# Signed-square keys, the last variance on VectorE, a late set of eight tiles and a fixed order table in a two-layer linear-attention kernel

## The chip, the cores and the metric

The kernel runs on one core of one Trainium2 chip. The metric is the device time of one execution in microseconds (us). Most statements below rest on one profiled execution of each kernel, whose span runs from its first to its last instruction. The span is shorter than the device time by about 1.8 us for the kernel before. PE is TensorE, DVE is VectorE, ACT is ScalarE, POOL is GpSimd, and SP is the engine whose queue issues most of the transfers.

## The reference

The input is x, 2048 tokens of 512 values in bf16. Four blocks follow one another, each applied to a layer-normalised x and added to x: linear attention, experts for two tokens, and the same two again with the same weights.

```python
def _A_ref(x, wqkv, wo):                       # linear attention, 32 heads of 16
    q, k, v = split(x @ wqkv)
    phi = lambda t: where(t > 0, t + 1, exp(t)) + 1e-6
    pq, pk = phi(q), phi(k)
    kv = einsum("bhsd,bhse->bhde", pk, v)      # summed over all tokens
    z = einsum("bhsd->bhd", pk)
    o = einsum("bhqd,bhde->bhqe", pq, kv) / (einsum("bhqd,bhd->bhq", pq, z)[..., None] + 1e-6)
    return merge(o) @ wo

def _B_ref(x, w_r, w_gate, w_up, w_down):      # two tokens of 2048
    r = x @ w_r
    idx = argsort(-r)[:2]
    y = (silu(x[idx] @ w_gate) * (x[idx] @ w_up)) @ w_down * sigmoid(r[idx])
    return x + scatter(y, idx)

x = x + _A_ref(layernorm(x)); x = x + _B_ref(layernorm(x))
x = x + _A_ref(layernorm(x)); x = x + _B_ref(layernorm(x))
```

As written, the router sees the normalised x, and its two winners need the scores of all tokens. So the kernel ends with a chain of small steps: the last tile's variance, the last keys, the top two, the gathering of two rows, two small products, and the store of the two rows.

## The kernel before

x lies in 16 tiles of 128 tokens. Every piece of work is an `op` on one engine, with a duration assumed. A planner sorts the ops, and each engine then runs its own list in that fixed order.

```python
class Plan:
    WEIGHTS = {'phi_raw0': -3.7, 'kw_one0': 3.8, ...}       # priorities; cut

    # loads, all on SP's queue but for wk; 'after' is the planner's earliest time
    for k in range(0, NC, 2):
        dma(wk[:, k : k + 2, :], A_wk[:, k : k + 2, :], [("wk", k)], 256, eng="ACT")
    ...
    for dst, src, key, kb, after in ((wq, A_wq, "wq", 512, 8.0), (wr, B_wrc, "wr", 1, 9.0), (wot, A_wot, "wot", 512, 30.0),
                                     (wv, A_wv, "wv", 512, 30.0 + 0.5), (wo, A_wo, "wo", 512, 30.0 + 3.0)):
        dma(dst[:], src, [key], kb, after)

    def trans(t):      # the normalised tile, transposed by a transfer on SP's queue
        nc.sync.dma_start_transpose(out=xnT[:, :, t * P : (t + 1) * P], in_=xn[:, t, 0:D])

    def Q(n):          # one quarter of the queries of four tiles: needs wq and four transposed tiles
        for i in range(NC):
            T_.matmul(p()[:], lhsT=wq[:, i, c, :], rhs=xnT[:, i, j * D : (j + 1) * D], start=(i == 0), stop=(i == NC - 1))

    def O(layer, t):   # one output tile; the very last one in three column parts of one PSUM tile
        cuts = [0, 256, 384, 512] if split else [0, D]
        ...            # DVE then adds it to x and sums the row in the same instruction
        # last tile: three squares on ACT, small sums on DVE, then Ln and Exp on ACT give rho = 1/sqrt(var)

    def lin(lo, hi):   # router scores of tiles lo to hi; rc is the score before the division by the deviation
        tiny([lambda: V.tensor_tensor(out=key_hi(1)[:, lo:hi], in0=rc[:], in1=rho[:, 2, lo:hi], op=ALU.mult)], ...)

    topk(1, 0, 12)     # top-8 of the early twelve tiles, beside the last output tiles
    for _ in range(12):        # dummy matmuls that keep PE busy beside the chain
        pe(MM, lambda: T_.matmul(sp_()[:], lhsT=warm[:, 0:P], rhs=warm[:], start=True, stop=True), ...)
    topk(1)            # then the top-8 of all
    # output tiles 4 to 15 scaled on ACT, DVE and POOL; three stores of four tiles; the row's store waits for all
```

Of the kernel before, what the change touches and what calls it, by code (L numbers as in the profile page):

```python
# [16 lines left out]
P = 128  # L17
# [4 lines left out]
NF = 11  # L22
# [3 lines left out]
XW = 544  # L26
G3 = 3 * P + 1
# [22 lines left out]
class Plan:  # L50
# [3 lines left out]
    WEIGHTS = {'phi_raw0': -3.7, 'kw_one0': 3.8, 'kv1': -2.2, 'den1': -3.8, 'mid_chain0': -4.9, 'lin1': 2.2, 'consts0': 5.8, 'phi0': 0.9, 'row_sums0': -8, 'K0': -0.9, 'O1': -0.3, 'copy_ps0': 5.0, 819: -3.0, 6: 0.7, 223: -0.4, 619: -0.7, 'mid': -8, 662: -1.5, 154: 1.5, 461: -0.7, 567: 0.7, 312: -0.4, 702: -0.7, 'stats0': 2.6, 601: -0.4, 378: 0.3, 725: -6.3, 789: -4.5, 879: -2.6, 215: 0.7, 660: -3.7, 231: -0.3, 430: -1.1, 67: -3.3, 21: -3.0, 186: 2.7, 917: -3.0, 630: 4.5, 765: -3.0, 448: 1.5, 271: -4.5, 393: 3.0, 788: -1.5, 416: -3.0, 419: 3.0, 650: -2.3, 937: -0.7, 701: -5.2, 10: -3.0, 354: 1.5, 148: 1.5, 474: 2.7, 793: 0.8, 'copy_ps1': 8, 812: -0.7, 610: -0.8, 606: 3.0, 53: -1.0, 598: 0.3, 208: -1.2, 516: -3.0, 76: 0.7, 205: -0.7, 749: -3.0, 56: -3.4, 54: -0.8, 119: -2.2, 411: -0.3, 684: 0.3, 335: 0.7, 83: 3.7, 623: 0.3, 863: -0.7, 743: -0.7, 90: 2.7, 944: -0.8, 198: 3.0, 434: 0.3, 338: 1.5, 132: 0.4, 278: 0.3, 490: 1.1, 925: 3.0, 717: -3.0, 676: 3.0, 364: -0.7, 697: -0.7, 563: 2.0, 848: -0.3, 535: 0.3, 802: -0.7, 435: 0.0, 636: -0.8, 572: 1.2, 446: 0.3, 821: -0.7, 918: -2.7, 342: 2.4, 907: -3.0, 674: -3.0, 503: -0.3, 898: -3.0, 501: 0.3, 740: 1.2, 605: 0.7, 578: -0.7, 806: -2.7, 203: -0.3, 589: -1.5, 835: -3.0, 417: -1.5, 665: -3.0, 813: 3.0, 596: 3.7, 399: -2.7, 333: -3.7, 551: -3.0, 107: -0.4, 562: 0.0, 649: 3.0, 872: 3.0, 458: -1.5, 887: -1.5, 382: 3.0, 451: 1.5, 428: 0.7, 373: 0.3, 582: 3.0, 96: 0.0, 44: 1.0, 785: 0.0, 645: -6.7, 934: 0.7, 940: -6.0, 'den0': -3.2, 576: 0.7, 'finish_sums1': -6.8, 423: -0.7, 168: 0.0, 844: -1.5, 685: -3.3, 415: -1.8, 309: 1.5, 149: -4.4, 719: -0.4, 926: 2.7, 518: 1.5, 282: 3.0, 62: 1.5, 1: 1.5, 185: -0.7, 392: 3.0, 306: -0.4, 212: 0.7, 60: 2.2, 337: 1.5, 447: 1.5, 5: -0.3, 396: 1.8, 838: 3.0, 164: -3.0, 363: 0.3, 126: -1.0, 478: -0.3, 300: -1.0, 395: 4.5, 742: 0.7, 55: 2.3, 626: -1.5, 460: 0.7, 873: -0.3, 497: 1.5, 664: -2.2, 261: 3.0, 110: 0.7, 173: 0.0, 866: -0.3, 573: 1.4, 269: -0.7, 521: -0.7, 255: 3.8, 721: 0.4, 699: -0.7, 'finish_sums0': -2.1, 339: 0.7, 520: 1.5, 877: -1.9, 588: 3.0, 616: -3.3, 170: -0.7, 943: 4.8, 557: 3.0, 360: 0.3, 193: 0.3, 496: -3.0, 723: 0.3, 250: -0.3, 45: 0.0, 317: 2.7, 58: -1.5, 900: 0.3, 194: -1.5, 542: 0.3, 529: 2.2, 919: 3.0, 239: 0.7, 522: 1.5, 407: -0.3, 651: 0.7, 449: 0.3, 804: 1.5, 608: 0.3, 669: 0.3, 483: -1.5, 914: -1.5, 754: 0.7, 859: -1.5, 'pre0': -2.7, 539: 3.0, 268: 4.8, 675: 0.7, 408: -1.5, 618: -0.7, 289: 1.5, 182: -0.7, 519: -0.8, 498: 1.0, 481: -4.5, 655: -0.3, 889: -1.0, 575: -0.3, 493: 1.5, 155: -2.3, 99: -1.4, 121: -0.7, 15: 3.7, 343: -2.2, 196: -0.7, 784: 0.4, 199: 0.7, 29: -0.3, 341: 0.3, 648: -3.7, 307: 3.3, 657: -3.0, 732: -0.7, 923: 0.7, 677: 2.2, 35: -1.5, 219: 1.8, 241: -0.8, 752: 3.3, 320: -1.5, 875: -3.0, 318: -0.3, 913: 3.0, 147: -1.5, 111: -1.5, 127: -0.7, 191: -2.2, 'phi_raw1': -0.9, 642: -0.6, 604: -3.0, 748: 0.7, 14: -0.3, 113: 3.0, 'topk1': 2.8, 262: 0.3, 144: -0.7, 172: 0.8, 210: 0.7, 105: -1.5, 667: -3.0, 506: -4.0, 'K_raw0': -1.9, 505: -0.3, 64: -0.3, 178: -0.3, 492: 0.3, 703: 0.3, 455: -0.7, 308: 1.5, 477: 0.7, 175: 0.3, 874: -1.5, 566: -4.5, 673: -0.7, 'Q1': -0.7, 'tail': 8, 254: -4.5, 187: -0.7, 264: 3.0, 97: 1.5, 927: -0.8, 183: 0.7, 776: 0.3, 592: 3.0, 329: -0.3, 'trans0': -6.7, 201: -3.0, 357: 0.8, 544: -0.8, 729: 1.5, 'gate_up0': 1.8, 'kw_one1': 4.5, 870: -2.1, 'mid_chain1': -3.5, 437: -0.3, 26: -0.3, 310: -0.6, 641: 0.3, 162: 1.8, 163: -1.8, 'last_scales1': 2.7, 607: 0.0, 422: -0.7, 74: 1.5, 'norm0': 0.7, 824: 3.0, 823: 0.7, 560: 0.3, 643: 0.3, 348: -3.0, 902: -0.3, 769: -3.0, 32: 0.7, 114: 0.7, 495: 0.7, 843: 2.3, 204: 3.0, 820: 0.7, 627: -0.3, 160: -3.0, 248: -0.3, 893: 3.0, 355: 3.0, 895: 3.7, 425: -0.7, 694: -0.3, 771: -1.5, 671: 3.0, 892: -3.0, 728: -0.3, 661: 0.7, 758: -2.2, 756: 0.7, 837: 0.3, 894: -0.3, 726: -0.3, 30: 0.3, 753: 0.3, 847: -0.3, 230: 0.7, 293: -0.3, 577: 0.7, 'logits0': -4.8, 359: 3.0, 849: -0.3, 406: 0.7, 181: 1.5, 540: 0.7, 140: 1.5, 871: -0.3, 603: -3.7, 450: 2.3, 635: 0.3, 901: 2.7, 561: 0.3, 639: -0.3, 381: 0.3, 34: -0.7, 731: -1.5, 23: -3.0, 757: 0.3, 600: 0.7, 376: -0.7, 922: 1.5, 27: 1.5, 243: -0.7, 103: -1.5, 779: -0.7, 897: 3.0, 825: 0.8, 445: 1.8, 'gate_up1': 7.2, 509: 3.0, 883: -0.7, 750: -1.5, 180: 3.0, 'picks0': -3.3, 273: 0.3, 693: -1.5, 854: 1.5, 558: -0.3, 939: -0.7, 475: 0.3, 20: 0.6, 'trans1': -2.5, 397: 0.7, 'rstd1': 0.3, 'rstd0': -1.0, 724: -3.0, 85: -0.7, 713: 0.7, 286: -3.0, 876: -0.7, 152: 1.5, 532: 1.5, 'patch': -1.2, 936: 0.7, 543: -0.3, 547: 0.3, 517: 1.5, 195: -0.3, 28: -0.3, 564: 3.0, 'picks1': -0.2, 385: -3.0, 375: -0.7, 916: 0.7, 534: -0.7, 9: 0.7, 'logits1': -2.7, 794: 0.3, 690: -3.0, 624: -3.0, 712: 3.0, 18: 0.3, 384: -1.2, 'K_raw1': 3.0, 799: 3.0, 891: -3.0, 700: -0.7, 292: 2.7, 476: 0.7, 'kv0': 2.7, 334: 3.0, 167: -0.7, 297: 0.7, 380: 0.3, 294: -3.0, 'wk_center0': -1.4, 68: -3.0, 109: 1.5, 369: 0.3, 862: 3.0, 770: -1.5, 511: -0.3, 'norm1': -1.5, 311: -3.0, 25: -1.5, 'O0': -0.7, 761: -3.0, 929: 1.5, 546: 3.0, 453: 3.0, 'phi1': 3.0, 734: -3.0, 766: -3.0, 41: -3.0, 256: -0.7, 244: 0.7, 'last_scales0': 1.5, 814: 0.3, 464: 0.7, 'Q0': 0.7, 512: -1.5, 344: -0.7, 358: -0.7, 429: 3.0, 'K1': 0.7, 670: 0.7, 508: -2.7, 510: -0.3, 'lin0': 0.7, 480: 0.3, 533: 0.7, 'stats1': 3.0, 161: -3.0, 'G1': 0.3}  # L54
    LAT = {"PE": 0.21, "ACT": 0.16, "DVE": 0.14, "POOL": 0.1, "SP": 2.7}

    def __init__(self, slots):
        self.ops, self.wrote, self.read, self.free = [], {}, {}, dict(slots)
        self.n, self.side, self.lazy, self.bias, self.kind = 0, False, 0.0, 0.0, ""

    def op(self, eng, dur, fn, r=(), w=(), hold=(), lat=None, prio=0.0, port=False):
        prio += self.bias + self.WEIGHTS.get(self.kind, 0.0) + self.WEIGHTS.get(self.n, 0.0) + 1e-4 * self.n
        o = Op(eng, dur, self.LAT[eng] if lat is None else lat, fn, prio, port)
        self.n += 1
# [50 lines left out]
    def order(self):  # L115
        ready = []
# [13 lines left out]
        while left:  # L130
# [15 lines left out]
            if o.kb:  # L146
                bw = max(bw, o.done) + o.kb / 284.0
                o.done = bw
            elif o.queue:
                o.done = max(o.done, bw + 0.5)  # L150
# [24 lines left out]
def linear_attention_moe(  # L175
# [37 lines left out]
    xt = big.tile([P, NC, NR * P], BF16, name="xt")  # L213
# [14 lines left out]
    def dma(dst, src, keys_, kb, after=0.0, eng="SP", **k):  # L228
        e = nc.sync if eng == "SP" else nc.scalar
        o = op(eng, 0.5, lambda: e.dma_start(out=dst, in_=src), w=keys_, lat=1.7, **k)  # L230
        o.kb, o.avail = kb, after
# [4 lines left out]
    def xt_load(lo, hi, after=0.0, **k):  # L236
        dma(xt[:, :, lo * P : hi * P], A_xt[:, :, lo * P : hi * P], [("xt", t) for t in range(lo, hi)], 128 * (hi - lo), after, **k)

    for k in range(0, NC, 2):
        dma(wk[:, k : k + 2, :], A_wk[:, k : k + 2, :], [("wk", k)], 256, eng="ACT")  # L240
    op("ACT", 1.28, lambda: nc.scalar.preload_act_table_set("natural_log_exp_and_others"), w=["table"])
    for i, (load, lo, hi, after) in enumerate((
        (x_load, 0, 2, 0.0),
        (xt_load, 0, 2, 0.0),
        (x_load, 2, 4, 0.0),
        (xt_load, 2, 4, 0.0),
        (x_load, 4, 6, 0.0),
        (xt_load, 4, 6, 0.0),
        (x_load, 6, 8, 5.0), (xt_load, 6, 8, 5.0), (x_load, 8, 12, 3.5),
    ) + tuple((xt_load, lo, min(lo + 4, NR), 11.0) for lo in range(8, NR, 4)) + ((x_load, 12, 16, 13.0),)):  # L250
        load(lo, hi, after, prio=-50.0 + i)
# [85 lines left out]
    def dve(dur, fn, **k):  # L337
        return op("DVE", dur, fn, **k)
# [1220 lines left out]
```

## Time and profile before

| | |
|---|---|
| median of three executions | 158.29 us (157.55 to 159.09) |
| profiled span | 156.9 us |
| first query product | 25.52 |
| first output product of the second layer | 124.00 |
| end of the last output product on PE | 142.33 |
| sum of tile 14 read on DVE (D14) | 141.55 |
| last top-8 starts (K) | 145.60 |
| row's store issued | 153.72 |

The rows from the third on are times from the span's start in the profiled execution. D14 and K are used throughout: D14 is when VectorE has read the row sums of the last full tile, and K is when the last top-8 starts. From the page come the busy time of each engine and the row of granted PE clock in 40 equal slices, in tenths of full speed:

```profile
PE 147.9 (94%) x1380; PEld 74.4 (47%) x1380; DVE 130.2 (83%) x481; ACT 111.9 (71%) x272; POOL 28.5 (18%) x78
PEclk9999999999999999999999999999999999999996
```

From about 12 us to the end of the outputs PE is idle only in short gaps, and its granted clock is 1.00 from 12 to 150 us. DVE is nearly as full at the end: the chain of what ended last runs over DVE from 128.10 to 141.90 us, with small gaps. The prediction shows the waits and the rest of the chain. This profiled execution took 158.73 us; spans of other executions of this kernel lie between 155.4 and 157.5 us. So a difference between two kernels in the milestones below, which compares one execution of each, carries some half a microsecond of scatter.

### The profile page before, as it was taken

To read this page: it belongs to the slowest core of one execution; us is meant where nothing else is said; L and a number is where in the kernel's file an instruction comes from. 1 tells how busy PE (TensorE), PEld (TensorE's weight loads), DVE (VectorE), ACT (ScalarE), POOL (GpSimd) and SP (SyncE) were. 2 spreads that over 40 slices of the span, in tenths; PEclk is the share of its full clock that TensorE was granted. 3 is DMA by queue.
4 is the path that set the end of the run, shared out by engine and by line. 5 is a ranking of instruction groups with operands and counts; after the bars stand their busy time and mean duration, and the time that the engine had idled before them with its cause. 6 is when DMAs were issued, how large, how long until landed. Compare 5 with 4: busy or idle time off the path is not lost.

```text
span 156.9 us, 3902 instructions
## 1 busy us (share of the span) xinstructions
PE 147.9 (94%) x1380; PEld 74.4 (47%) x1380; DVE 130.2 (83%) x481; ACT 111.9 (71%) x272; POOL 28.5 (18%) x78
## 2 busy tenths in 40 slices
PE   6989999997999999999999999999999999998970
PEld 2434444443454444444545545576444455465660
DVE  1799999776699999999999979853488999999840
ACT  3379999653567788799978657712478998898930
POOL 7801055100000000120321000300430000643200
PEclk9999999999999999999999999999999999999996
DMA  3999846549998000033144530000000000030570
GB/s 103 355 355 322 241 97 71 102 100 289 439 437 340 3 4 0 0 69 67 38 102 100 105 67 6 0 4 0 0 4 0 4 0 0 4 136 2 174 231 2
DMA packets 24499, 17.15 MB, mean 109 GB/s; under 512 B 17952, under 2 KB 22560, under 8 KB 24096
## 3 DMA queue, kind: packets, MB, share of 16 engines
q1 hardware_dynamic: 24184, 16.39, 35.7%
q10 hardware_dynamic: 296, 0.53, 0.9%
q8 instruction: 10, 0.16, 0.4%
q14 instruction: 9, 0.07, 0.2%
HBM read 10.62 MB, written 2.10 MB: 81 GB/s over the span
## 4 chain that ended last, share of the span: by engine, by line
PE 72%; DVE 12%; DMA 5%; ACT 5%; issue 3%; SPq 0%; ACTq 0%; DVEq 0%
PE mm L487 18%; PE g L473 17%; PE g L618 11%; PE mm L441 10%; DVE x L628 4%; PE mm L454 4%; DMA wv<-in_A_wv_dram 3%; ACT pk L1334 3%; DMA x<-in_A_x_dram 3%; DVE st L358 2%; DVE pq L604 2%; PE tp L581 1%; PE tp L1059 1%; PE g L563 1%; PE mm L597 1%
## 5 line engine op out<-in xcount | busy, mean ns | idle before, releaser
L408 ACT ACTIVATE e<-mm 128x512 bf16<-128x512 f32 x52 | 30.4, 597 | 12.7 <-PE mm L441 6.7
L473 PE MATMUL g<-pk,xn 128*128 128x512 bf16 x128 | 32.0, 379 | 0.4 <-DVE pk L432 0.4
L487 PE MATMUL mm<-xnT,wq 128*128 128x512 bf16 x128 | 31.9, 379 | 0.0
L618 PE MATMUL g<-KW,pq 128*128 128x512 bf16 (+2 forms) x136 | 30.6, 366 | 0.4 <-DVE x L628 0.4
L636 ACT ACTIVATE sq<-x 128x512 bf16<-128x512 bf16 (+2 forms) x34 | 20.4, 601 | 2.9 <-DVE x L628 2.5
L441 PE MATMUL mm<-wk,xnT 128*128 128x512 bf16 x80 | 19.9, 379 | 0.0
L473 PEld LDWEIGHTS <-xn 128*128 128x128 bf16 x128 | 12.1, 98 | 15.9 <-issue 2.5
L618 PEld LDWEIGHTS <-pq 128*128 128x128 bf16 x136 | 12.7, 98 | 13.8 <-issue 0.5
L412 DVE TENSOR_SCALAR em<-e 128x512 bf16<-128x512 bf16 x52 | 15.1, 297 | 3.7 <-ACT e L408 3.5
L487 PEld LDWEIGHTS <-wq 128*128 128x128 bf16 x128 | 11.4, 97 | 12.5 <-issue 0.8
L394 POOL TENSOR_SCALAR xn<-x,s,nb 128x512 bf16<-128x512 bf16 x6 | 4.9, 825 | 52.9 <-PE g L618 37.9
L419 DVE SCALAR_TENSOR_TENSOR pk<-mm,em 128x512 bf16<-128x512 f32 x20 | 13.7, 687 | 0.3
L358 DVE BATCH_NORM_STATS2 st<-x 128x6 f32<-128x512 bf16 x16 | 10.4, 666 | 3.3 <-DMA x<-in_A_x_dram 3.3
L628 DVE SCALAR_TENSOR_TENSOR x<-x,opr,g 128x512 bf16<-128x512 bf16 (+2 forms) x18 | 11.9, 684 | 0.4 <-PE g L618 0.3
L441 PEld LDWEIGHTS <-xnT 128*128 128x128 bf16 x80 | 7.4, 98 | 8.9 <-DMA xnT<-xn 0.5
L628 DVE SCALAR_TENSOR_TENSOR x<-x,g 128x512 bf16<-128x512 bf16 x16 | 10.9, 683 | 0.7 <-PE g L618 0.3
L419 DVE SCALAR_TENSOR_TENSOR pq<-mm,em 128x512 bf16<-128x512 f32 x16 | 10.7, 685 | 0.1
L411 ACT ACTIVATE rl<-mm 128x512 bf16<-128x512 f32 x16 | 9.4, 612 | 1.8 <-DVE pq L416 1.0
L604 DVE TENSOR_TENSOR pq<-pq,rd 128x1024 bf16<-128x1024 bf16 x16 | 10.4, 686 | 0.0
L454 PE MATMUL mm<-wkc,xt 128*128 128x512 bf16 x40 | 10.1, 379 | 0.3 <-ACT rl L428 0.3
L427 ACT ACTIVATE e<-mm,rho 128x512 bf16<-128x512 f32 x12 | 8.2, 683 | 1.2 <-PE mm L460 1.1
L373 ACT ACTIVATE lnv<-mv,eps_t 128x2 f32<-128x2 f32 (+3 forms) x18 | 5.2, 291 | 5.0 <-DVE mv L359 3.3
(263 smaller groups left out, 232.1 us busy)
## 6 DMA issues: line engine op xcount, KB each, us to landing
wgu<-in_B_wgu_dram SPq DMA_DIRECT2D x2, 1408.0 KB, 13.6
out_dram<-pk SPq DMA_DIRECT2D x4, 512.0 KB, 4.0
wd<-in_B_wd_dram SPq DMA_DIRECT2D x1, 1408.0 KB
x<-in_A_x_dram SPq DMA_DIRECT2D x4, 256.0 KB, 5.2
xt<-in_A_xt_dram SPq DMA_DIRECT2D x4, 256.0 KB, 5.3
x<-in_A_x_dram SPq DMA_DIRECT2D x2, 512.0 KB, 5.6
wk<-in_A_wk_dram ACTq DMA_DIRECT2D x2, 256.0 KB, 4.1
wq<-in_A_wq_dram SPq DMA_DIRECT2D x1, 512.0 KB, 6.8
```

The lines of the kernel that those rows point to most:

```text
L358: dve(0.61, lambda: V.bn_stats(out=st()[:], in_=x[:, t, :]), r=[("x", t)], w=[st]).early = 4.0
L408: act(0.5, lambda: A.activation(out=e()[:], in_=p()[:], func=ACT.Exp), r=[p], w=[e], **k)
L412: dve(0.2, lambda: V.tensor_scalar(out=em()[:], in0=e()[:], scalar1=1.0, scalar2=TINY, op0=ALU.min, op1=ALU.add), r=[e], w=[em], port=True ...
L419: dve(0.6, lambda: V.scalar_tensor_tensor(out=out_ap, in0=p()[:], scalar=0.0, in1=em()[:], op0=ALU.max, op1=ALU.add), r=[p, em], w=[key], **k)
L441: T_.matmul(p()[:], lhsT=xnT[:, c, t * P : (t + 1) * P], rhs=wk[:, c, :], start=(c == 0), stop=(c == NC - 1))
L454: T_.matmul(p()[:], lhsT=xt[:, c, t * P : (t + 1) * P], rhs=w[:, c, :], start=(c == 0), stop=(t >= NM and c == NC - 1),)
L473: T_.matmul(Gs[c]()[:], lhsT=xn[:, t, gcol(c) : gcol(c) + P], rhs=pk[:, t, :], start=first, stop=last)
L487: T_.matmul(p()[:], lhsT=wq[:, i, c, :], rhs=xnT[:, i, j * D : (j + 1) * D], start=(i == 0), stop=(i == NC - 1))
L604: dve(0.6, lambda q=q: V.tensor_tensor(out=q, in0=q, in1=rd()[:].to_broadcast([P, 2, D]), op=ALU.mult), r=[rd], w=[("pq", j, c), ("pq", j, ...
L618: T_.matmul(p()[:, a : a + n], lhsT=pqt(c, t * P, P), rhs=KWs[layer][:, c, a : a + n], start=(c == 0), stop=(c == NC - 1),)
L628: dve(0.04 + 0.6 * n / D, lambda q=q, a=a, n=n: V.scalar_tensor_tensor(out=x[:, t, a : a + n], in0=x[:, t, a : a + n], scalar=1.0 if i == ...
L636: act(0.1 + 0.5 * n / D, lambda q=q, a=a, n=n, sq=sq: A.activation(out=sq()[:, 0:n], in_=x[:, t, a : a + n], func=ACT.Square, scale=float( ...
```

## The change

The intent was to close PE's two gaps, to shorten the chain behind the last tile, and to keep DVE and POOL apart in ops that the code marks `port`: in the kernel before, one clamp of 128x512 took 1.04 us on DVE at 27.29, beside memsets on POOL, where the nine others of its line took 0.25 to 0.29. The core of the diff, cut:

```diff
-    WEIGHTS = {'phi_raw0': -3.7, ...}
+    WEIGHTS = {}
+    TIMES = [0.7, 1.2, 1.7, 0.8, ..., 12.9234, 13.9234, 17.0434, 13.4236, ...]   # one start time for each op
     def order(self):
+        if self.TIMES:
+            for o in self.ops:
+                o.start = self.TIMES[o.n]
+            return sorted(self.ops, key=lambda o: o.start)
...
-    xt = big.tile([P, NC, NR * P], BF16, name="xt")
+    xt = big.tile([P, NR // 2, NC, 2 * P], BF16, name="xt")
...       # wk in two halves on two queues, x 0-1 second on ACT's queue
-    QA, QT = 3, 8
+    QA, QT = 4, 6
...       # port=True on some two dozen more ops: the table was made with DVE and POOL apart in those
-        cuts = [0, 256, 384, 512] if split else [0, D]
+        cuts = [0, 320, 512] if split else [0, D]
+        parts = [(i, a, b - a, ps("g")) for i, (a, b) in enumerate(zip(cuts, cuts[1:]))]
...       # the last part's sum of squares on DVE; variance vv without ACT
+            tiny([
+                lambda: V.scalar_tensor_tensor(out=r2[:], in0=rc[:], scalar=-1.0, in1=rc[:], op0=ALU.mult, op1=ALU.max),
+                lambda: V.tensor_tensor(out=r2[:], in0=r2[:], in1=rc[:], op=ALU.mult),
+            ], r=[("rc", lo)], w=[("r2", lo)])
+            tiny([lambda: V.reciprocal(out=iv[:], in_=vv[:])], r=["vv"], w=[("iv", lo)])
+            tiny([lambda: V.tensor_tensor(out=key_hi(1)[:, lo:hi], in0=r2[:], in1=iv[:], op=ALU.mult)], ...)
...       # key = rc*|rc|/var: the same order as rc/sqrt(var), with no Ln and Exp
-    lo, LE = ORD[12], (0, 12) if ORD[12] == 12 else (4, 16)
+    lo, LE = ORD[12], (0, L0)          # L0 = 8: early set 0-7, late set 8-15
...
-        pe(MM, lambda: T_.matmul(sp_()[:], lhsT=warm[:, 0:P], rhs=warm[:], start=True, stop=True), ...)
+        pe(0.11, lambda: [
+            T_.matmul(sp_()[:], lhsT=warm[:, 0:P], rhs=warm[:, 0:P], start=True, stop=True) for _ in range(2)
+        ], ...)
...       # gather in two halves; gate, up and down products in parts; Silu's table load earlier
```

The times of the table decide only the order.

## The prediction

> **What bounds the kernel now.** I read the page first: TensorE (PE) is busy 94% of 156.9 us, VectorE (DVE) 83%, ScalarE (ACT) 71%, GpSimd (POOL) 18%. A mean over stages decides nothing, so next came the table of busy time by stretches (start, busy us and count per engine, PE clock, DMA share, GB/s).
>
> ```profile
> 8.00:12.00 4.00, 3.37 (x16) 1.35 (x15) 4.00 (x13) 2.94 (x7) 0.09 (x1) 1.00 1.10 359
> 12.00:30.00 18.00, 18.00 (x85) 8.16 (x84) 17.55 (x59) 16.94 (x37) 6.11 (x10) 1.00 0.74 169
> 34.00:39.00 5.00, 3.87 (x19) 1.70 (x18) 3.94 (x9) 2.40 (x5) 0.00 (x0) 1.00 0.79 233
> 132.00:142.00 10.00, 9.60 (x96) 5.47 (x95) 10.00 (x45) 8.84 (x29) 5.05 (x15) 1.00 0.16 55
> 150.00:157.00 7.00, 2.12 (x88) 1.60 (x83) 1.56 (x9) 0.56 (x3) 0.00 (x0) 0.80 0.26 86
> ```
>
> There are three stages. Until 12 us loads, DVE and PE wait for each other. From 12 to 142 us PE is never idle but for two gaps. After 142 us a chain of small steps runs to 156.9: 15 us in which no engine is the bound. "Busy" alone can mislead for pipelined matmuls, so I checked the chain of work: there a group of four 512-column matmuls takes 0.86 us, 0.216 each, one after another through the whole middle. No reordering shortens that; it can only close gaps. PE's waits name all gaps over 0.35 us:
>
> ```profile
> PE tp L792 <- DMA wv<-in_A_wv_dram: 1.1, 1, 1.1
> PE g L1482 <- issue: 0.6, 1, 0.6
> PE g L1482 <- DVE h L1470: 0.5, 1, 0.5
> PE g L618 <- DVE x L628: 0.4, 1, 0.4
> PE g L473 <- DVE pk L432: 0.4, 1, 0.4
> ```
>
> The first, at 38 us, is the load of wv, issued only at 34.29 behind DMA transposes and landing 4.6 us later. The fourth, at 141.95, is the last O tile: its three column parts share one PSUM tile. The end of the chain (start us, us, what):
>
> ```profile
> 142.37 0.50 DVE x L628 x2
> ...
> 143.65 0.29 ACT sq L636 x2
> ...
> 144.80 0.30 ACT lnv L657
> 145.11 0.02 issue
> 145.13 0.20 ACT rho L660
> 145.33 3.52 ACT pk L1334 x5
> 148.86 0.02 issue
> 148.88 1.28 ACT L1447
> 150.16 0.01 issue
> 150.17 0.21 ACT s L1448
> ...
> 151.64 0.69 PE g L1482 x36
> 152.32 0.57 issue
> 152.89 0.32 PE g L1482 x8
> ```
>
> The last key needs the last tile's variance, so a square, a Ln and an Exp on ACT precede it. The timeline has the key product (L700) at 145.40 and the local top-8 (L974) at 145.60. ACT then scales five output tiles and only afterwards loads the Silu table.
>
> [...] the same clamp of 128x512 bf16 takes 350 ns in 12 to 30 us, with GpSimd a third busy, and 287 ns in 40 to 60 us, with GpSimd idle. [...] Here the load takes 1283 ns and Tanh starts 1.29 us after its beginning[...]. [...] The trace has 355 to 361 GB/s while loads saturate and 317 to 348 during the stores.
>
> **The change part by part.**
>
> *Start.* wk goes on two queues ahead of x, so the first statistics should start about 1 us later than the present 4.79. In return DVE loses work before the first pk: blockmask (0.66), casts (0.3), an xn now on GpSimd (0.39), and the order puts K of tile 7 in front of G of tile 0, where PE now waits 0.4. xt comes in 2 KB runs instead of 512 B, but loads already run at 355 GB/s. One spin less lies before work that waits for wk anyway. I count 0, give or take 0.5.
>
> *Middle.* The same matmuls of 0.216 us. The table puts wv's load ahead of wot, and the matmul that needs it well over 5 us after it: more than the 4.6 us of landing. **−1.1 us.** The last O tile gets one PSUM tile per part: **−0.4 us.** [...] Against this, DVE (17.55 of 18, and 10.0 of 10) and ACT (16.94 of 18) have hardly any slack, and all engines run a new fixed order, worked out with assumed durations. I allow **+0.5 us** of new stalls.
>
> *From tile 14 to the last keys.* Tile 14's sum ends on DVE at 141.55; the top-8 starts at 145.60, 4.05 us later. After: two x parts of 320 and 192 columns (from the rows 0.34, 0.48 and 0.74 us for 128, 256 and 512 columns, 0.08 for each accumulator: 0.63 + 0.49), mean 0.2, square-sum of 192 columns on DVE 0.5, variance 0.25, reciprocal 0.2, key 0.2, and 0.3 for the sums of tiles 12 to 14 in between (a dependent small DVE step is 0.2 from start to start, an independent one 0.1). That is 2.8; ACT's square of tile 14 and of the first part fit beside it. Ln and Exp leave this path. **−1.25 us.**
>
> *From the top-8 to the final store.* Before: top-8 at K = 145.60, row store issued at 153.72, K + 8.12. After, by engines: the top-8 over partitions 0.2 sooner, as a warm-up matmul no longer blocks it (K to the index compare 1.45, not 1.68); compare to gather 0.22; two half gathers of 16 matmuls, 0.45 each, because the late set is 8 tiles, not 4, though the add of the first half hides; gate matmuls from about K + 2.7 (was K + 3.02) with 1.29 to the first DVE step, 0.44 to Silu. So Silu starts near K + 4.4 (was K + 4.75). The steps from Silu to the down projection shrink from 1.29 to about 1.1 and the down projection comes in two parts. The up projection's second half ends near K + 5.1 and allows its share of the down projection at K + 5.7; it ends near K + 6.4, the row is ready near K + 6.7, and the store could go at K + 6.95. The 0.57 us "issue" hole inside the down projection may recur: K + 7.5. The table load moves off ACT's output queue, but Silu's input is ready at 150.31 against a table at 150.16, so this alone gives nothing.
>
> The row store must also wait for the four tile stores. Before, three of 512 KB go out at 146.12 to 148.9, and their data flow from 147 to 151.6:
>
> ```profile
> 147.00:148.00 1.00, 0.92 (x19) 0.50 (x17) 0.97 (x8) 1.00 (x2) 0.17 (x1) 1.00 0.96 317
> 150.00:151.00 1.00, 1.00 (x44) 0.97 (x39) 0.73 (x6) 0.56 (x3) 0.00 (x0) 1.00 1.03 348
> 151.00:152.00 1.00, 0.51 (x32) 0.37 (x34) 0.54 (x4) 0.00 (x0) 0.00 (x0) 1.00 0.70 224
> ```
>
> 1.5 MB at 340 GB/s is 4.6 us. The new order lets the first of these three stores go about 1.4 us after the top-8 (before: 0.5), so they would land near K + 7.5. Both paths meet there: **−0.6 us** instead of −1.2. The store, landing and end of 3.2 us stay.
>
> Sum: −1.1 − 0.4 + 0.5 − 1.25 − 0.6 = −2.85; 158.29 − 2.85 = 155.4 us.
>
> **The rivals.** *A: the fixed order stalls PE.* For it: DVE, ACT and PE are all over 94% busy in 12 to 30 us, first statistics come later, and G now trails K by two tiles, not three. Against: G's order is free, the PSUM pools are unchanged, and PE already runs ahead of DVE by a buffer or two. It would cost 1 to 3 us and leave 156 to 158.5. *B: the output stores take the place of the chain.* For it: the 4.6 us of flow above, with only about 1 us of slack now, and the later first store. It would cap the gain after the top-8 at 0.3 to 0.6, as I assume half-way; were it absent, 154.8. *C: PE was the bound and the tail's gain is all there is*, because the wv gap is only moved (the following Q and G need what DVE has not finished; DVE is 3.94 of 5 busy around the gap): 156.5. *D: everything in the sum comes without new stalls and the issue hole goes too*: 153.7.
>
> **Range and chances.** A and C are the likelier departures upward, D downward. 8 in 10: 153.6 to 157.3. A gain of 2% needs 155.13, just below my figure, so faster and same are nearly even: faster 0.45, same 0.51, slower 0.04 (a stall of over 6 us would be needed to lose 2%).
>
> **What would show it.** PE's waits without wv, PE full from about 12 us, and tile 14's sum done near 140.5 instead of 141.55 would confirm the middle; a new PE wait on pk, xn or a PSUM buffer would show A. Top-8 2.8 us after that sum, with no Ln or Exp in between, confirms the keys. A last wait of the row store on the tile stores confirms B; a wait on yo refutes it. I am wrong if PE starts its full stretch over 1 us later, or if small steps on a full DVE queue up ahead of the key.

The sum is −2.85 us and so 155.4 us; a term of 0 is cut from it. That term was an estimate of mine from 350 and 287 ns: with DVE and POOL kept apart, some 60 ns less on each of 12 clamps and less on others, about 1 us of DVE in a stretch where PE is full, and so nothing for the whole. The load of 1283 ns is ACT's table load at 148.88. The durations in the part on tile 14 that were not measured as such (mean, square-sum, variance, reciprocal, key and sums) are estimates of mine from the steps measured there: 0.2 us for a small dependent one, 0.34 to 0.74 us for one of 128 to 512 columns.

## The result, and the profile after

The changed kernel is correct and took 164.14 us (median of 4 executions, 163.44 to 164.72), against 158.11 us for the kernel before in the same rounds (157.55 to 159.09, 4 executions). The ratio is 1.0372, with a 95% interval of 1.0303 to 1.0442: slower, and far outside the predicted range. A ratio here is the mean time of one kernel's fast runs over the mean of the other's of the same rounds, so it is not quite the ratio of the medians quoted. Executions over 1.5% slower than the fastest of the same kernel are left out of the means.

The profiled span grew from 156.9 to 161.5 us; the rest of the 6.0 us is taken up under e5. By milestones, in us from the span's start:

| | before | after | difference |
|---|---|---|---|
| first query product | 25.52 | 23.94 | |
| last output product ends on PE | 142.33 | 145.23 | +2.90 |
| D14, sum of tile 14 read | 141.55 | 146.30 | +4.75 |
| K, last top-8 starts | 145.60 | 149.65 | D14 to K: −0.70 |
| row's store issued | 153.72 | 158.40 | K to store: +0.63 |
| end | 156.90 | 161.51 | store to end: −0.07 |

The four steps from D14 on sum to the +4.6 us of the span. The page of the changed kernel, same two lines as before:

```profile
PE 148.8 (92%) x1370; PEld 75.9 (47%) x1390; DVE 132.6 (82%) x486; ACT 110.1 (68%) x266; POOL 31.9 (20%) x80
PEclk9999995999999999999999999999999999999998
```

The seventh slice of the clock row says 5: half speed from 24.12 to 27.54 us from the start. PE's waits in the changed kernel (engine, line, what it waited for: us in total, times, longest) name no wv any more, and no PSUM wait at the last tile:

```profile
PE mm L502 <- issue: 2.6, 2, 2.5
...
PE tp L602 <- DVE Z L534: 0.5, 1, 0.5
```

But a wait of 2.5 us stands in front of a query product (L502). "Issue" means that the profile found no releaser, so the transfers had to be looked at. The SP queue of the changed kernel (start, us, what, count):

```profile
14.57 2.57 SPq L417 DMA_TRANSPOSE xnT<-xn  x2
17.20 0.57 SPq L240 DMA_DIRECT2D wq<-in_A_wq_dram  x1
17.86 6.44 SPq L417 DMA_TRANSPOSE xnT<-xn  x5
```

In the kernel before, wq's load was issued at 6.98. Here it stands behind two more loads and three transposes, at 17.20, and lands at 22.23. The transpose of tile 2 is issued behind it at 17.86 and lands at 23.73, 5.9 us later; the median of such a transpose is 2.5 us. The first query product needs both, and starts at 23.94, where PE was ready at 21.48. The table by stretches shows what followed (start and end, length, busy us and count of PE, PEld, DVE, ACT and POOL, then granted PE clock, DMA share, GB/s):

```profile
22.00:23.00 1.00, 0.00 (x0) 0.00 (x0) 1.00 (x7) 0.78 (x2) 0.00 (x0) 1.00 1.97 132
...
24.00:25.00 1.00, 1.00 (x3) 0.34 (x4) 0.00 (x0) 0.00 (x0) 0.00 (x0) 0.56 1.23 253
25.00:26.00 1.00, 1.00 (x4) 0.43 (x3) 0.00 (x0) 0.32 (x1) 0.00 (x0) 0.50 0.09 18
26.00:27.00 1.00, 1.00 (x4) 0.33 (x3) 0.29 (x1) 1.00 (x4) 0.00 (x0) 0.50 0.00 0
```

After the gap PE is busy, but at half clock: four matmuls take 1.71 us, not 0.86. The end of the chain of waits (start, us, what) is the second finding:

```profile
141.90 2.00 DVE x L647 x6
143.90 0.60 DVE rho L740 x2
...
144.97 1.33 DVE x L647 x4
146.30 0.08 DVE s L1022
...
149.44 0.17 DVE keys L737
...
149.69 0.14 DVE s L1022
```

From 139.45 us to K every link of it is DVE. In the kernel before, PE's last output product was still a link at 141.95. D14 now comes 1.07 us after PE's last output product, where it came 0.78 us ahead of it. The third finding is a wait of SP for the stores of the tiles, ahead of the row's store:

```profile
SPq L1584 <- DMA out_dram<-pk: 1.1, 1, 1.1
```

The row was ready at 157.09; its store went at 158.40.

### The profile page after: what moved, and what is told of

It reads as the page before. It is cut to its first block, busy times and chain, and to the rows that moved or that the text cites. A ratio compares the mean times of both kernels' runs of the same rounds, so it can differ in the third digit from the quotient of the medians.

```text
span 161.5 us, 3881 instructions
## 1 busy us (share of the span) xinstructions
PE 148.8 (92%) x1370; PEld 75.9 (47%) x1390; DVE 132.6 (82%) x486; ACT 110.1 (68%) x266; POOL 31.9 (20%) x80
## 4 chain that ended last, share of the span: by engine, by line
PE 68%; DVE 21%; DMA 3%; issue 3%; ACT 1%; ACTq 0%; DVEq 0%
PE mm L502 16%; PE g L488 14%; PE g L637 14%; PE mm L456 11%; DVE st L373 4%; DMA x<-in_A_x_dram 3%; DVE x L647 3%; PE tp L602 2%; DVE pk L447 1%; PE tp L1107 1%; PE g L584 1%; PE mm L618 1%; DVE em L444 1%; PE mm L469 1%; PE tp L757 1%
## 5 line engine op out<-in xcount | busy, mean ns | idle before, releaser
L502 PE MATMUL mm<-xnT,wq 128*128 128x512 bf16 x119 | 32.5, 388 | 3.0 <-issue 2.6
L637 PE MATMUL g<-KW,pq 128*128 128x512 bf16 (+2 forms) x128 | 29.1, 372 | 0.3 <-issue 0.2
L657 ACT ACTIVATE sq<-x 128x512 bf16<-128x512 bf16 x31 | 19.1, 622 | 0.4 <-DVE x L647 0.4
L502 PEld LDWEIGHTS <-wq 128*128 128x128 bf16 x128 | 11.5, 100 | 15.9 <-issue 5.0
L409 POOL TENSOR_SCALAR xn<-x,s,nb 128x512 bf16<-128x512 bf16 x6 | 5.7, 952 | 51.3 <-PE mm L618 39.4
L409 POOL TENSOR_SCALAR xn<-x,rho,nb 128x512 bf16<-128x512 bf16 x9 | 7.2, 802 | 17.2 <-DVE nb L396 8.4
L443 ACT ACTIVATE rl<-mm,rho 128x512 bf16<-128x512 f32 x12 | 7.9, 684 | 1.5 <-PE mm L469 0.8
```

The source lines that it names most:

```text
L409: e.tensor_scalar(out=xn[:, t, 0:D], in0=x[:, t, :], scalar1=s_, scalar2=b_, op0=ALU.mult, op1=ALU.add)
L637: T_.matmul(p()[:, 0:n], lhsT=pqt(c, t * P, P), rhs=KWs[layer][:, c, a : a + n], start=(c == 0), stop=(c == NC - 1),)
L657: act(0.6, lambda: A.activation(out=sq()[:], in_=x[:, t, :], func=ACT.Square, scale=float(D) ** -0.5, accum_out=sums[:, i, 1, t : t + 1]), ...
```

## The experiments

Thirteen kernels ran, each against the kernel before on the same chip. All were correct but one. Two times that share no rounds are compared by their ratios to the kernel before. Entries of the order table are written as assignments.

**The gap at the first query product.** The theory: wq's place in the queue makes the gap, and the idleness of PE makes the half clock, two costs that can be told apart. The rival: the order table itself loses the time elsewhere.

```diff
-TIMES[14] = 17.0434      # load of wq
+TIMES[14] = 6.3
```

> The changed kernel with one entry of its order table moved: the load of wq goes out with the other early loads (after x of tiles 8 to 11) instead of at 17.2 us, behind two more loads and three transposes. Theory (late loads): in the changed kernel Q of group 0 waits until 23.94 us for the transpose of tile 2, which was queued behind wq's 512 KB and landed 5.9 us after its issue (the median is 2.5). With wq early, wq lands by 15 us and that transpose by about 20.5, before TensorE is ready at 21.5: the 2.5 us gap and the 3.4 us at half clock both go, about -4.2 us: 160.0 us, span 157.4. Rival (TensorE is waiting for VectorE or for a PSUM buffer there, or the transposes are slow by themselves): the gap stays above 1.5 us and the time above 162.5.

Measured: 161.19 us (160.90 to 161.50), ratio 1.0183 (1.0133 to 1.0233), span 158.0. The first query product starts at 21.76, and no half clock follows: the one in the tail, below, and that from 155.5 us on make up the mean of 0.981. The span fell by 3.5 of the 4.6 us by which it had grown, and D14 by 3.70 of 4.75 us. A single entry of the table is thus most of the loss in span, and about half of it in device time (1.9 of the 3.7% in ratio). The expected 160.0 us and span of 157.4 were missed by 1.2 and 0.6 us.

```diff
+    # 13 dummy matmuls of 512 columns ahead of the first query product
+    pe(2.8, lambda: [T_.matmul(ws()[:], lhsT=warm[:, 0:P], rhs=warm[:], start=True, stop=True) for _ in range(13)], w=[ws])
```

> The changed kernel with 13 matmuls on a zero tile (2.8 us of TensorE) put right in front of the first Q, so that TensorE is busy while the transposes are still on their way. Nothing else is moved. Theory (the half clock from 24 to 27.4 us is a consequence of TensorE's idleness[...]): the granted clock stays at 1.00, the first Q still starts at about 24.1, and the time falls by 1.5 to 1.7 us to 162.5. Rival (the clock drops for another reason): the clock still falls to 0.5 near 24 us and the time is 164.2 or a little more.

Measured: 162.48 us (162.37 to 162.60), ratio 1.0267 (1.0219 to 1.0315), span 160.5. The query product starts even later, at 24.51, yet the first query group after it runs at a granted clock of 1.00, and D14 comes 1.06 us sooner than in the changed kernel. The stretch that has half clock in the changed kernel (0.56, three matmuls in 1 us) was here

```profile
24.00:25.00 1.00, 1.00 (x7) 0.45 (x5) 1.00 (x3) 0.00 (x0) 0.00 (x0) 1.00 1.02 205
```

The stall remained and its consequence went. With 0.57 us lost at the start of the queries and 1.06 won at D14, the half clock was worth about 1.6 us, by one profiled execution of each kernel.

In the changed kernel's one profiled execution PE had 0.50 of its clock from 24.12 to 27.54 us, after 2.46 us without a matmul.

```diff
-TIMES[14] = 17.0434      # load of wq
+TIMES[14] = 17.6         # behind the transpose of tile 2
```

> The changed kernel with the load of wq moved back by one place in the queue, behind the transpose of tile 2. This tells which of the two transfers holds the first Q. Theory (the transpose of tile 2 is the last to arrive because it stands behind wq): that transpose now lands at about 20, wq at about 22.8 to 23.5, and the gap shrinks from 2.5 us to 1.3 to 2.0; [...] the time lies between 160.5 and 164. Rival (wq's own landing is what counts and it is delayed by transposes): wq lands later than now and the gap grows to 3 us or more, time 164.5 or more.

Measured: 162.14 us (161.50 to 162.48), ratio 1.0230 (1.0178 to 1.0282), span 159.3. In its trace the transpose of tile 2 now lands at 20.28, 3.2 us after its issue, and PE waits for wq alone:

```profile
PE mm L502 <- DMA wq<-in_A_wq_dram: 1.9, 1, 1.9
```

The clock stayed at 1.00 after this gap of 1.9 us in the profiled execution, where it fell after 2.46 us in that of the changed kernel. Over the whole span its mean was 0.996 there and 0.972 to 0.981 in the other three executions, so in those it fell somewhere, and no trace of them is kept: 1.9 us is not shown to be always safe. Swapping the two transfers takes the wait of the one and leaves that of the other. Only wq stood too far back: ahead of it, the transpose of tile 2 lands before PE is ready at about 21.4; it was late in the changed kernel, 5.9 us from issue to landing instead of 3.2, because it stood behind wq.

```diff
-key = r2 * iv            # rc*|rc| / var
+key = rc * rho           # Ln and Exp on ACT back on the path of the key; in short: so for all tiles
```

> The changed kernel without the signed-square keys: the key is again the row sum times rho, so the last key waits for Ln and Exp on ScalarE; the squares and the reciprocal on VectorE are left out, everything else stays in its place (for the last key: one place later). Theory of my prediction (Ln and Exp are what the signed square takes off the path): the last top-8 starts 0.5 to 0.6 us later, measured from the end of tile 14's sum, and the time rises by about 0.5 us. Rival (reciprocal, two products and the wait between them cost VectorE about what Ln and Exp cost ScalarE): the top-8 starts within 0.25 us of where it did, 3.1 to 3.6 us after tile 14's sum, and the time does not move by more than the scatter.

Measured: 162.39 us (161.01 to 164.33), ratio 1.0230 (1.0163 to 1.0297). The profiled execution was slow, with half clock on PE from 150.2 us on, so only the stretch ahead of that is compared: D14 to K took 3.53 us, against 3.35 with the signed squares. By this one pair of profiles, one of them slow, the squares are worth 0.18 us, the rival's figure: four small DVE steps and a reciprocal replace Ln and Exp. The time fits neither theory: the fast executions, without the squares, took 161.01 to 162.66 us with spans of 159.0 to 160.1, where the changed kernel's spans are 161.4 to 161.8, and the intervals of the two ratios do not overlap. The two ran in different rounds. The only trace of e4, the slow one, has the same wait ahead of the first query product (2.8 us by its table of waits, 2.5 in the changed kernel) and D14 at 146.21 us, against 146.30. So why the fast ones are shorter stays open, and with it what the squares cost or gain in the whole. As wq is as late in e4 as in the changed kernel, and the intervals of e1 and e4 overlap, the worth of wq's entry rests on the traces and spans, not on device times alone.

**The tail, POOL beside DVE, and the other way round.** e5 to e7 keep wq early.

```diff
-    for _ in range(12): two matmuls of 128 columns
+    for _ in range(12): one matmul of 512 columns        # as in the kernel before
```

> Early wq as in e1_wq_early (161.19 us, span 158.0), and in addition the kernel before's twelve dummy matmuls of 512 columns in place of twenty-four of 128. Theory: the short dummies let TensorE's granted clock fall to 0.5 in the tail of e1 (145.6 to 148.6 us), and that cost some 0.3 us there; with long ones the granted clock is 1.00 from tile 14's sum to the gate projection, the last top-8's start is as in e1 (145.96 within 0.2), the row is ready 7.4 to 7.6 us after it (8.72 in e1), and the time is 160.7 to 161.0, because the row's store then waits for the tile stores. Rival: the short clock fall is chance and costs nothing; the time stays at 161.2 within 0.2, or the longer dummies stand in the key path's way and it gets 0.2 to 0.5 worse.

In e1, two stretches of the tail, with the columns as above, were

```profile
145.00:146.00 1.00, 1.00 (x26) 0.95 (x24) 0.97 (x10) 0.85 (x4) 0.71 (x4) 0.63 0.08 28
146.00:147.00 1.00, 1.00 (x8) 0.96 (x7) 0.97 (x6) 1.00 (x2) 0.57 (x1) 0.50 0.00 0
```

and in e5 the second of them was

```profile
146.00:147.00 1.00, 1.00 (x8) 0.81 (x7) 0.97 (x5) 1.00 (x3) 0.30 (x1) 1.00 0.00 0
```

Measured: 159.61 us (159.39 to 160.22), ratio 1.0104 (1.0071 to 1.0137), span 157.4. The row was ready 7.27 us after K instead of 8.72. The theory holds for the clock. The time fell by more than either theory said, 0.8% in ratio, because the span is not all of it: the device time exceeded the span by 3.0 to 3.5 us in three of four executions of e1, and by 1.9 to 2.0 in all of e5. What that extra microsecond is stays open. It appeared in executions of the changed kernel (2 of 4), e1, e3 and e4, in none of e2 and e5 to e9 nor of the kernel before (at most 2.0 us in 47 executions), and in one or two executions each of e10 to e13. Nor do short dummies lower the clock of the tail in every kernel: in the profiles of the changed kernel and of e2 and e3, which have them too, it stayed at 1.00 there. In e1 it fell although no wait of PE after 141 us exceeded 0.80 us; matmuls took 2.08 us of the stretch from 142.20 to 145.60 (mean clock 0.95). In e5 they took 2.24 us of 142.00 to 145.40, and it stayed at 1.00; in the changed kernel 2.08 us of 145.90 to 149.30, as in e1, and it stayed too.

```diff
-TIMES[934] = 144.7704    # output tile 6 on ACT, behind tiles 10 and 9
+TIMES[934] = 143.3105
-TIMES[936] = 145.5504    # store of tiles 4 to 7, behind that of 8 to 11
+TIMES[936] = 144.9
```

> e5_dummies_512 with ScalarE's output tile 6 ahead of tiles 10, 9 and 12 instead of behind 10 and 9, and the store of tiles 4 to 7 ahead of that of 8 to 11. Theory: in the changed kernel the row's store waits 1.3 us for the tile stores, because the first of the last three leaves 1.38 us after the last top-8's start; with tile 6 early it leaves 0.5 us after it or sooner, the row's store waits less than 0.4 us, and the time is 0.7 to 0.9 us below that of e5_dummies_512. Rival: the three last stores are bound by the last tile (VectorE's 13 to 15) alone, and the time stays within 0.2 us of e5_dummies_512.

Measured (on top of e5): 159.11 us (158.29 to 160.26), ratio 1.0084 (1.0043 to 1.0124), span 156.6. The first of the three stores leaves 0.60 us after K instead of 1.33, SP's wait for the tile stores falls from 1.0 to 0.4 us, and the row's store is issued at K + 7.84 instead of K + 8.58. In the profile the theory holds. In the ratio its 0.7 us do not show beyond the intervals.

```diff
-TIMES[676], TIMES[679] = 113.3274, 115.0774   # POOL adds two expert rows to x
+TIMES[676], TIMES[679] = 112.75, 112.76       # ahead of its copy of two queries
```

> e5_dummies_512 with GpSimd's two patches of x in the key-value stage of the second layer placed ahead of its copy of the patched queries, as the kernel before has them, so that they are over before VectorE's router correction. Theory: that correction takes 1.29 us where the kernel before takes 0.51[...]; behind it stand the mask of Z, the masked key-value product, the denominators and VectorE's whole backlog. With the patch early it takes 0.5 us again, TensorE's wait of 0.50 us ahead of the denominators goes, the first output of the second layer starts at 122.8 to 123.0 instead of 123.48, tile 14's sum is read 0.6 to 0.8 us earlier, and the time falls by 0.6 to 0.8 us below e5_dummies_512. Rival: the end is set by VectorE's count of work from 124 us on (18.8 us against 17.4 in the kernel before), and the tile 14 sum moves by less than 0.2 us.

Measured (on top of e5): 159.79 us (159.05 to 160.93), ratio 1.0126 (1.0087 to 1.0166), span 157.2: no gain. The timelines of DVE (start, us, line, operation) say why. In e5

```profile
115.61 1.29 DVE L1329 SCALAR_TENSOR_TENSOR nrr<-eq,s,nrr 128x16 f32<-128x16 f32 x2
```

and in e7

```profile
112.42 0.82 DVE L427 TENSOR_SCALAR em<-e 128x512 bf16<-128x512 bf16 x1
113.61 1.12 DVE L1285 TENSOR_SCALAR s<-s 128x8 f32<-128x8 f32 x1
116.31 0.51 DVE L1329 SCALAR_TENSOR_TENSOR nrr<-eq,s,nrr 128x16 f32<-128x16 f32 x2
```

The router correction is back at its 0.51 us, as expected. But two other DVE instructions now run beside POOL's patch, which lasts from 111.94 to 114.70. They take 0.82 instead of 0.28 and 1.12 instead of 0.17 us, and the next step stands where it stood. The first output product of the second layer came 0.09 us sooner, not 0.5: the rival won, for a reason that it did not name.

The second instruction of the router correction took 1.02 us in e5, ending at 116.90 where POOL's patch ended at 116.87, and 0.24 in e7, where the patch was over. Not every DVE instruction beside the patch was slowed: the one at 113.27 in e7 took 0.43 us, as at 112.72 in e5 without it. What decides this no run shows. The order table was made to keep DVE and POOL apart in the ops marked `port`, but it fixes an order on each engine and no time between two engines.

```diff
 # the kernel before, with one load moved after planning
+    todo.remove(wv_op)
+    todo.insert(todo.index(todo_sp[at - 2]), wv_op)     # two transposes earlier
```

> The kernel before with one thing moved: the load of wv is issued ahead of the last two transposes instead of behind them (31.7 instead of 34.3 us). Theory: TensorE's wait of 1.1 us for wv goes, everything after it comes 1.0 us earlier, span 155.9, time 157.1, ratio 0.993 to 0.994. Rival: the two transposes behind 512 KB of wv land some 3 us later, as the transpose of tile 2 did behind wq in the changed kernel, the keys of tiles 14 and 15 wait for them, and the time stays within 0.3 us of 158.1.

Measured: 158.37 us (157.95 to 158.80), ratio 1.0006 (0.9981 to 1.0032), span 157.0. The wait for wv is gone, and a new one stands in its place:

```profile
PE mm L443 <- DMA xnT<-xn: 0.8, 1, 0.8
```

The rival holds. In either kernel the transposes behind a 512 KB load in one queue came late: in the changed kernel one landed 5.9 us after its issue, where the median is 2.5, and here PE waits 0.84 us, until 36.43, for transposes that were issued behind wv from 32.57 on.

**Why VectorE is late at the end.** All on top of e6.

```diff
-TIMES[725] = 115.9734    # a query product, behind the denominators that wait for Z
+TIMES[725] = 115.66      # ahead of them
```

> e6_tile6_first with one swap on TensorE in the second layer's key-value stage: a query product that waits for nothing goes ahead of the denominators that wait for Z (0.50 us in all of the changed kernel's runs). Theory: VectorE's backlog at the end (tile 14's sum read 1.1 us after the last output product instead of 0.8 us before it) comes from queries made too late; the swap fills the wait, brings the first output product from 123.09 to 122.6 and tile 14's sum from 142.22 to 141.8 or sooner, and the time falls by 0.4 to 0.5 us below e6_tile6_first. Rival: VectorE is full from 120 us on and takes the query when it can; tile 14's sum moves by less than 0.15 us and the time by less than 0.2 us.

Measured: 159.13 us (158.45 to 161.18, the last slow), ratio of the fast runs 1.0030 (0.9964 to 1.0095), span 156.7. The wait of 0.50 us went, but the first output product came at 123.07 instead of 123.09 and D14 at 142.21 instead of 142.22. By the profile the rival holds; the ratio is lower, in other rounds and with a wide interval.

```diff
 # e9, and
-    COPYK[14] = 'DVE'
+    COPYK[14] = 'ACT'    # one PSUM copy of 0.69 us
```

> e9_query_before_den with one PSUM copy of 0.69 us in the second layer's key-value stage taken from VectorE and given to ScalarE. Theory: from there to tile 14's sum VectorE is the engine that is full (idle 0.3 us of 19), so 0.69 us less for it brings that sum 0.5 to 0.7 us earlier, and the time falls by as much below e9_query_before_den. Rival: ScalarE is as full there (3.9 of 4 us between 120 and 124), the exponentials that VectorE waits for come later by the same 0.6 us, and the sum moves by less than 0.2 us.

Measured: 159.80 us (158.89 to 160.95), ratio 1.0095 (1.0022 to 1.0169), span 157.2. D14 came 0.65 us later than in e9, with the first output product 0.65 us later: the copy was on the way to that product, and ACT reached it late. The theory falls.

```diff
-TIMES[796, 797, 798, 935, 937] = 136.3154 ... 143.3404   # POOL's output tiles
+TIMES[796, 797, 798, 935, 937] = 146.02 ... 146.06       # behind the last top-8
...       # three more entries moved (799, 936, 941), the stores of these tiles among them
```

> e6_tile6_first with all five output tiles of GpSimd moved behind the last top-8 ([...]the tile stores come late on purpose, so the time itself gets worse by 1 to 4 us). Theory: VectorE's small instructions that fall on a GpSimd output lose up to 0.5 us each; without those outputs the pair of router products that took 0.68 us takes under 0.2 us, tile 14's sum is read 0.5 to 0.7 us earlier than 142.22, and the last top-8 starts at 145.0 to 145.2 instead of 145.64. Rival: [...]both move by less than 0.15 us.

Measured: a single execution of 162.63 us, of unknown state, and a wrong result (relative error 0.297), by my mistake: the store of tiles 8 to 11 stayed ahead of output tile 8 in the order. The stretch up to K is not touched by that. There the pair of router products (L740) took 0.26 instead of 0.69 us, and D14 came 0.62 us after PE's last output product instead of 1.08. K came 4.02 us after that product instead of 4.50.

**Fourth job.**

```diff
 # e9, and two query products with their ACT and DVE work earlier
-TIMES[742], TIMES[747] = 120.5294, 119.6574
+TIMES[742], TIMES[747] = 111.7975, 110.2775
```

> e9_query_before_den with two query products of the second layer, and the ScalarE and VectorE work on them, moved from just ahead of the first output product (119.7 and 120.5 in the order table) to the stage before, where VectorE has 1.3 us idle in every 4. TensorE's sum of work is the same. Theory: from 120 us on VectorE is full and is what sets tile 14's sum (1.08 us after the last output product in every run of this family, 19.1 us after the first one; 17.55 in the kernel before, which had done more of the scaling of the queries by then); with 1.1 us of it done earlier the sum is read 0.4 us or less after the last output product, the last top-8 starts 0.5 to 0.9 us sooner than e9's 145.63, and the time is 158.2 to 158.7, 0.4 to 0.8 below e9_query_before_den. Rival: the key-value chain that these queries stood beside now leaves TensorE waiting, the first output product comes 0.3 us later or no sooner than the sum of work allows, and the time stays within 0.3 us of e9_query_before_den's 159.1.

Measured: 161.46 us (160.07 to 162.64, one of six slow), ratio 1.0230 (1.0190 to 1.0270), span 158.4. The second layer's key-value product starts at 118.29 instead of 116.26, and around it PE now waits 0.3, 0.4 and 0.8 us for ACT and DVE, so the first output product comes at 124.69 instead of 123.07. D14 is still 1.07 us behind the last output product. The theory expected a shorter lag from moving this work ahead of 120 us, and that did not come; but as new waits opened, the run does not say where the lag is made.

What was still open was what POOL's work beside DVE costs of that lag, with a right result.

```diff
 # e9, and
-TIMES[531] = 135.9156    # three memsets on POOL, 0.8 us, ahead of its first outputs
+TIMES[531] = 116.5       # where it stands idle
```

> e9_query_before_den with GpSimd's three memsets (0.8 us) moved from just ahead of its first output tiles to where it stands idle, 20 us before; nothing else. Theory: GpSimd's outputs 1 and 2 then end at 139.7 instead of 140.4, VectorE's pair of router products (0.69 us for two, 0.26 us where no output of GpSimd ran beside it) takes 0.26 us, tile 14's sum is read 0.4 us earlier (0.65 us after the last output product instead of 1.08), the last top-8 starts 0.3 to 0.4 us earlier against the last output product, and the ratio to the kernel before falls from 1.003 to 0.999 to 1.001. Rival: GpSimd's later outputs move up too and hit VectorE's next small instructions, as in e7_patch_first; the sum still comes 0.9 to 1.1 us after the last output product and the ratio stays at 1.003 or above.

POOL's outputs 1 and 2 and DVE's router products, in e9,

```profile
138.87 1.53 POOL L1385 TENSOR_SCALAR pk<-x,opr,nb 128x512 bf16<-128x512 bf16 x2
139.71 0.69 DVE L740 TENSOR_TENSOR rho<-s,rho 128x4 f32<-128x4 f32 x2
```

and in e13

```profile
138.32 1.53 POOL L1385 TENSOR_SCALAR pk<-x,opr,nb 128x512 bf16<-128x512 bf16 x2
139.68 0.25 DVE L740 TENSOR_TENSOR rho<-s,rho 128x4 f32<-128x4 f32 x2
```

Measured: 158.21 us (157.94 to 159.40), ratio 1.0028 (0.9995 to 1.0062), span 156.3. The longer of the two router products took 0.59 us in e9 and 0.18 in e13. D14 comes 0.66 us after the last output product instead of 1.09, and K 4.02 us after it instead of 4.51. The theory holds in the profile to the hundredth. The ratio did not follow it below 1.0030, but the interval of e9 is too wide to say whether it moved.

No version beat the kernel before. With five repairs the changed kernel stands level with it: 158.21 against 158.08 us in the same rounds.

## Why the prediction was wrong, point by point

The largest error is **the allowance of +0.5 us for new stalls in the middle**. The runs put in its place a gap of 2.46 us and a half clock worth about 1.6 us (e2): 4.1 us. e1, which undoes both, moves the span by 3.5 and D14 by 3.70. I had checked where the table puts wv's load against its consumer, and not where it puts wq's. The row was in the diff: its entry is 17.04, behind the loads at 12.92 and 13.92. In all the sum was off by 7.5 us of span (−2.85 against +4.6): 5.75 of them up to D14, 0.55 from D14 to K, 1.2 from K to the store. Of the 5.75, 3.70 are the entry of wq (e1); the other 2.1 are the gains that did not reach D14, taken up below. I thought of one stall of over 6 us as the only way to a loss of 2% and gave it 4 in 100; it came from several errors at once.

**Start, 0 give or take 0.5.** Not contradicted. The first statistics start at 6.26 instead of 4.79, later than I said, and the first product of the first group at 12.66 instead of 11.71; but one key product of 0.86 us is then done that came behind it before.

**wv, −1.1.** The wait vanished as predicted, but it did not reach the end. In e6, where wq is early, the second layer's key-value product starts at 116.03 instead of 116.33: 0.3 of the 1.1. The rest is not assigned to single waits. e8 shows the same in the kernel before: the gap can be moved and the time not. That is rival C.

**DVE and POOL apart, 0 in the middle.** The 350 ns of the clamp that I read there is a mean: of the ten clamps at L429 between 12 and 30 us one took 1.04 us, at 27.29, beside memsets on POOL, and the other nine 0.25 to 0.29. So 60 ns on each was no fair reading. Where POOL's work beside DVE did cost something, 0.43 us at the end (e13), I had no term for it.

**Last output tile, −0.4.** The wait on PSUM is gone, as I said; its worth is not isolated. In e1 PE ends the last output product 0.80 us sooner than in the kernel before, but 0.54 us of router products that stood ahead of it there now stand behind it. And the term was in the wrong place: the wait, at 141.95, came after D14 (141.55), so to close it could not bring D14 forward. It lay within the 4.05 us that I shortened by 1.25.

**The step that I did not have: D14 follows PE.** I took 141.55 − 1.1 − 0.4 + 0.5 to put tile 14's sum near 140.5. In e1, e5, e6, e7 and e9, with wq early, it comes at 142.2 to 142.6, some 1.1 us after the last output product, where it was 0.78 us ahead. VectorE has become the bound of the last stretch: it led the chain there before too, but with gaps. Of that lag 0.43 us went when POOL's memsets were moved away (e13). The remainder was not taken apart by a run; the changes upstream in e9, e10 and e12 did not remove it. By count in the traces, between the first output product and D14 VectorE has one scaling of 0.69 us and two query products of 0.85 us in all more in e9 than in the kernel before, and that stretch is longer by 1.6 us (19.14 against 17.55). This fits, but no run separates it. The prediction named the sign itself: small steps queueing up on a full DVE.

**Tile 14 to the keys, −1.25.** The direction was right and the size was off: 3.35 us instead of 4.05, so −0.70, where I reckoned with 2.8. No Ln and Exp stand on the path. Their absence is worth only 0.18 us, by e4's one trace.

**Top-8 to the row's store, −0.6.** Wrong in sign in the changed kernel: +0.63. Gate products start at K + 2.94 instead of the K + 2.7 that I expected, Silu at K + 4.83 instead of K + 4.4, and the row is ready at K + 7.44 instead of K + 6.7. The chain was thus 0.5 us shorter than before (K + 7.93), not 1.2. Rival B then took more than that: the row's store waited for the tile stores. Repaired in e13, it is issued at K + 8.07, against K + 8.12 before: nothing won.

**The rivals.** A was right in kind, as the fixed order did stall PE, but on a transfer queue and not on pk, xn or PSUM, and at 3.5 to 3.7 us (e1) where I gave it 1 to 3. B held. Of C the part on wv held (e8), but the gain of the tail on which its 156.5 us rested did not come. D did not occur.

## What to carry to other kernels

In a fixed order, check for every load how late it may be issued and what is queued behind it: one entry of nearly a thousand cost 3.5 us of span here, and the transpose behind a load of 512 KB landed 5.9 us after its issue, where the median is 2.5. A planner's table keeps an order, not a time, so two engines that are apart in the table can meet on the chip (e7: a DVE step of 0.28 us took 0.82 beside POOL); shift whole blocks into idle time, as with the memsets, rather than rely on small gaps. Before counting a step as saved, ask which engine ends last in that stretch once it is gone, and look at the clock in every stretch where work was made shorter (0.50 in e1's tail).
